# A fused Fourier filter and MLP kernel: d transform split by the parity of d, W staged raw and copied forwards and backwards on chip

One core of one Trainium2 chip. The metric is the device time of one execution in microseconds (us). "Span" is the part of it between the first and the last instruction of the profile; the rest, about 1.7 us (135.18 - 133.5 in the profiled run of the kernel before), lies outside. A core alone has no second die to compare with; a run counts as slow when it is over 1.5% above the fastest of the same kernel.

## What must be computed

```python
def reference(A_x, A_w_r, A_w_i, B_x, B_w1, B_b1, B_w2, gate_w):   # x: 1 x 2048 x 512, bf16
    x = A_x
    g = sigmoid((x * gate_w).sum(-1, keepdims=True))
    a = irfft2(rfft2(x) * (w_r + 1j * w_i))          # w_r, w_i: 2048 x 257
    h = x @ w1 + b1                                  # w1: 512 x 1792
    b = (h * tanh(softplus(h))) @ w2                 # w2: 1792 x 512
    return g * a + (1 - g) * b
```

The program is two jobs that share the engines: a Fourier chain and an MLP. The Fourier chain is: t transform by 16 x 128 in two steps (s1, s2), d transform (a1), product with W, and the same backwards (s2i, s1i, a1i). Between s1/a1 and s2, and again between s2i and s1i, the data go through a scratch array in DRAM. The two MLP products are mm1 (x by w1) and mm2 (by w2).

## The kernel before

A list scheduler fixes the order on every engine when the kernel is built, from guessed durations. A task is taken when its inputs are guessed to be ready, highest priority first. So an input that lands later than guessed stops the engine although other work is ready. All loads but one tiny one are issued from SyncE (queue "sp").

```python
def dma(name, dst, src, nbytes, reads=(), writes=(), deps=(), ..., queue="sp", bw=DMA_BW):
    t = G.add(name, [(queue, 0.46, lambda e: e.dma_start(dst, src))], reads=reads, writes=writes, deps=deps, ...)
    t.xfer = nbytes / bw            # the guess of the transfer's time

ld_x(0, 1, bw=600e3); ld_x(1, 2, bw=260e3)
ld_w1(0)                            # 256 columns of w1
ld_x(2, 4, bw=290e3)
ld_w1(1)                            # 256 more
ld_c(0, ...); ld_w1(2); ...         # tables, and the other 1280 columns

def wload(nm, dst, src_t, o, h, deps=()):          # half h of w_r or w_i
    v = src_t.rearrange("(g h e2 j) k -> g h e2 j k", g=16, h=2, e2=2)
    part("p", 0, dst[0:32, j0:j0 + n, :]..., v[:, 0, :, j0:j0 + n, :]..., 32 * 514 * n, 188e3)
    # ... the mirrored rows: 16 partitions each, rows of 257 elements in reverse order
wload("wr", Wa, A_w_r, "Wa", 0); wload("wi", Wb, A_w_i, "Wb", 0)
# after the first scratch writes are issued:
wload("wr", Wa, A_w_r, "Wa", 1, t_r1w); wload("wi", Wb, A_w_i, "Wb", 1, t_r1w)

def f_a1(e, t=t, sl=sl):                           # forward d transform of one tile
    e.matmul(o[:, :, 1::2, :], In1[:, t, 256:384], f4(256), start=True, stop=False)   # 256 columns
    e.matmul(o[:, :, 1::2, :], In1[:, t, 384:512], f4(512), start=False, stop=True)   # 256
    e.matmul(o[:, :, 0, :], In1[:, t, 0:128], f2(0), start=True, stop=True)           # 128
    return e.matmul(o[:, :, 2, :], In1[:, t, 128:256], f2(128), start=True, stop=True)  # 128
```

Note the source of the forward W load: its outermost dimension has 16 entries (g).

Of the kernel before, what the change touches and what calls it, by code (L numbers as in the profile page):

```python
# [7 lines left out]
BF = mybir.dt.bfloat16  # L8
# [9 lines left out]
NWARM = 14  # L18
# [5 lines left out]
BIDX = {t: i for i, t in enumerate(BGRP)}  # L24
# [7 lines left out]
def _bf16_bits(a):  # L32
# [8 lines left out]
        "SA0", "SA1", "SB0", "SB1", "SA0e", "SA1e", "SB0e", "SB1e")  # L41


def _pin(t, pl, c, e2):
    return t * 8 + pl * 4 + c * 2 + e2


def _pout(co, sg, g, e2):


    return co * 64 + (32 + 31 - g * 2 - e2 if sg else g * 2 + e2)


def _stage2():
    t = np.arange(16)
    w = lambda num, den: np.exp(-2j * np.pi * num / den)
    M = {n: np.zeros((128, 128)) for n in MATS}

    def put_c(mat, po, rows, vals):

        mat[rows, po[0]] += vals.real
        mat[rows, po[1]] += vals.imag

    for e2 in range(2):
        Rr, Ri, Ir, Ii = (_pin(t, pl, c, e2) for pl in (0, 1) for c in (0, 1))
        for g in range(16):
            wt = w(t * g, 16)
            po = [[(_pout(0, sg, g, e2), _pout(1, sg, g, e2)) for sg in range(2)]][0]
            for mat, ok in (("RF", True), ("RFe", e2 == 1)):
                if ok:  # L70
                    m = M[mat]
                    put_c(m, po[0], Rr, wt)
                    put_c(m, po[0], Ri, 1j * wt)
                    put_c(m, po[0], Ir, 1j * wt)
                    put_c(m, po[0], Ii, -wt)
                    cw = np.conj(wt)
                    put_c(m, po[1], Rr, cw)
                    put_c(m, po[1], Ri, -1j * cw)
                    put_c(m, po[1], Ir, 1j * cw)
                    put_c(m, po[1], Ii, cw)  # L80
            for mat, ok in (("RFz", True), ("RFez", e2 == 1)):
                if ok:
                    m = M[mat]
                    put_c(m, po[0], Rr, wt)
                    put_c(m, po[0], Ri, 1j * wt)
                    put_c(m, po[1], Ir, wt)
                    put_c(m, po[1], Ii, 1j * wt)
            if e2 == 0:
                w64 = w(64 * t, 2048) * w(t * (15 - g), 16)
                m = M["RFe"]  # L90
                put_c(m, po[0], Rr, wt)
                put_c(m, po[0], Ir, 1j * wt)
                put_c(m, po[1], Ri, w64)
                put_c(m, po[1], Ii, 1j * w64)
                m = M["RFez"]
                for x, (r0, r64) in enumerate(((Rr, Ri), (Ir, Ii))):
                    if g == 0:
                        m[r0, po[x][0]] += 1.0
                        m[r0, po[x][1]] += w(t * 8, 16).real
                    elif g < 8:  # L100
                        put_c(m, po[x], r0, wt)
                    else:
                        put_c(m, po[x], r64, w(64 * t, 2048) * w(t * (g - 8), 16))

    inv = {}
    for nm in ("", "e", "z", "ez"):
        inv[nm] = np.zeros((128, 128))

    def take(mat, po, col, vals):

        mat[po[0], col] += vals.real
        mat[po[1], col] += -vals.imag

    for e2 in range(2):
        Rr, Ri, Ir, Ii = (_pin(t, pl, c, e2) for pl in (0, 1) for c in (0, 1))
        for g in range(16):
            wt = np.conj(w(t * g, 16))
            po = [(_pout(0, sg, g, e2), _pout(1, sg, g, e2)) for sg in range(2)]
            for nm, ok in (("", True), ("e", e2 == 1)):
                if ok:  # L120
                    m = inv[nm]
                    take(m, po[0], Rr, wt / 2)
                    take(m, po[0], Ri, -1j * wt / 2)
                    take(m, po[0], Ir, -1j * wt / 2)
                    take(m, po[0], Ii, -wt / 2)
                    cw = np.conj(wt)
                    take(m, po[1], Rr, cw / 2)
                    take(m, po[1], Ri, 1j * cw / 2)
                    take(m, po[1], Ir, -1j * cw / 2)
                    take(m, po[1], Ii, cw / 2)  # L130
            for nm, ok in (("z", True), ("ez", e2 == 1)):
                if ok:
                    m = inv[nm]
                    take(m, po[0], Rr, wt)
                    take(m, po[0], Ri, -1j * wt)
                    take(m, po[1], Ir, wt)
                    take(m, po[1], Ii, -1j * wt)
            if e2 == 0:
                w64 = np.conj(w(64 * t, 2048) * w(t * (15 - g), 16))
                m = inv["e"]  # L140
                take(m, po[0], Rr, wt)
                take(m, po[0], Ir, -1j * wt)
                take(m, po[1], Ri, w64)
                take(m, po[1], Ii, -1j * w64)
                m = inv["ez"]
                for x, (r0, r64) in enumerate(((Rr, Ri), (Ir, Ii))):
                    if g == 0:
                        m[po[x][0], r0] += 1.0
                        m[po[x][1], r0] += w(t * 8, 16).real
                    elif g < 8:  # L150
                        take(m, po[x], r0, 2 * wt)
                    else:
                        take(m, po[x], r64, 2 * np.conj(w(64 * t, 2048)) * np.conj(w(t * (g - 8), 16)))
    for nm in ("", "e", "z", "ez"):
        m1 = inv[nm]
        M["RI1" + nm] = m1
        if "z" in nm:
            M["RI2" + nm] = np.concatenate([m1[64:128], m1[0:64]])

    for co in range(2):  # L160
        for e2 in range(2):
            for g in range(16):
                for x in range(2):
                    po = _pout(co, x, g, e2)
                    for suf in ("", "e"):
                        A, B = M[f"SA{x}{suf}"], M[f"SB{x}{suf}"]
                        if suf == "" or e2 == 1:
                            A[_pout(co, 0, g, e2), po] += 0.5
                            A[_pout(co, 1, g, e2), po] += 0.5
                            B[_pout(co, 0, g, e2), po] += 0.5  # L170
                            B[_pout(co, 1, g, e2), po] -= 0.5
                        elif g == 0:
                            A[_pout(co, 0, 8 * co, 0), po] += 1.0
                        elif g < 8:
                            A[_pout(co, 0, g, 0), po] += 0.5
                            A[_pout(co, 0, 16 - g, 0), po] += 0.5
                            B[_pout(co, 0, g, 0), po] += 0.5
                            B[_pout(co, 0, 16 - g, 0), po] -= 0.5
                        else:
                            h = g - 8  # L180
                            A[_pout(co, 1, 15 - h, 0), po] += 0.5
                            A[_pout(co, 1, h, 0), po] += 0.5
                            B[_pout(co, 1, 15 - h, 0), po] += 0.5
                            B[_pout(co, 1, h, 0), po] -= 0.5
    return np.stack([M[n] for n in MATS], axis=1)


def _build_consts():
    cs = {}
    n = np.arange(128)[:, None]  # L190
    q = np.arange(64)[None, :]

    def trig(nn, k):
        th = 2 * np.pi * nn * k / D
        return np.cos(th), -np.sin(th)

    c0, s0 = trig(n, 4 * q)
    s0[:, 0] = (-1.0) ** np.arange(128)
    c2, s2 = trig(n, 4 * q + 2)
    ko = np.concatenate([4 * q + 1, 4 * q + 3], axis=1)  # L200
    blocks = [c0, s0, c2, s2]
    for h in range(2):
        c1, s1 = trig(n + 128 * h, ko)
        blocks += [c1, s1]
    cs["FD"] = np.concatenate(blocks, axis=1)
# [3 lines left out]
    FT = np.zeros((128, NT, 128))  # L209
    GT = np.zeros((128, NT, 128))  # L210
    for t in range(NT):
        th = 2 * np.pi * e * (16 * p + t) / S
        FT[:, t, 0:64] = np.cos(th)
        FT[:, t, 64:128] = -np.sin(th)
        FT[:, t, 64] = (-1.0) ** p[:, 0]
        GT[0:64, t, :] = 2 * np.cos(th).T
        GT[64:128, t, :] = -2 * np.sin(th).T
        GT[0, t, :] = 1.0
        GT[64, t, :] = (-1.0) ** p[:, 0]
    cs["CF"] = np.concatenate([cs.pop("FD"), FT.reshape(128, NT * 128)], axis=1)  # L220
    cs["GT"] = GT


    GD = np.zeros((128, 768))
    n1, n2 = np.arange(128)[None, :], np.arange(256)[None, :]
    for i in range(2):
# [826 lines left out]
```

## Time and profile before

| | before |
|---|---|
| time, median of 3 runs | 135.45 us |
| span of the profiled run | 133.5 us |
| TensorE (PE) busy | 128.9 us, 97% |
| idle time of PE in the span | 4.6 us |
| longest waits of PE | 1.2 us (warm-up, on zeros), 0.6 us |
| first mm1 matmul | 6.70 us |
| first matmul of s2 / of s1i | 45.48 / 92.39 us |

Two things that the prediction does not show matter later. This is the view of the transfers of the kernel before: out<-in, queue, number, size, median us from issue to landing.

```profile
scr<-R SPq DMA_DIRECT2D x8, 512.0 KB, 4.0
...
w_sb<-in_B_w_dram SPq DMA_DIRECT2D x2, 256.0 KB, 3.9
```

The two first pieces of w1 land 3.9 us after their issue, and the scratch writes after 4.0. This is the timeline of SyncE in the middle: start, length, what.

```profile
27.84 4.73 SPq L495 DMA_DIRECT2D scr<-R  x3
32.61 1.95 SPq L495 DMA_DIRECT2D w_sb<-in_B_w_dram  x2
36.35 2.19 SPq L495 DMA_DIRECT2D R<-scr  x4
```

Both halves of w2 are issued by 34.6 us, ahead of the second half of W.

### The profile page before, as it was taken

Reading aid. Unit: us, or ns where it says so; the run is one execution under the profiler, and the core shown is the slowest. Engines: PE = TensorE matmul, PEld = TensorE weight load, DVE = VectorE, ACT = ScalarE, POOL = GpSimd, SP = SyncE. Lnnn points to the kernel's source line nnn. Section 1 sums busy time; section 2 is a strip of 40 time slices with the busy share of each in tenths; the row PEclk is TensorE's granted clock in tenths of the full one; section 3 lists DMA queues with packets and bytes.
Section 4 is the critical chain, followed back from the end, with each engine's and each line's share of the span. In section 5 each row is a group of like instructions: output and inputs, shape, how many; then the busy total and the mean of one; then the engine's idle time right before and its main releaser. Section 6 shows DMA issues by size and latency. Waiting matters only on the chain.

```text
span 133.5 us, 2357 instructions
## 1 busy us (share of the span) xinstructions
PE 128.9 (97%) x813; PEld 69.4 (52%) x813; DVE 99.4 (75%) x241; ACT 82.8 (62%) x145; POOL 4.7 (4%) x8
## 2 busy tenths in 40 slices
PE   6999999999999999999998999999999999999991
PEld 2489565675444444444443444445666566565451
DVE  0558868487999799999999995001899999977822
ACT  3199788896774156756167898778887654552000
POOL 2000000000002900000000000000000000000000
PEclk9999999999999999999999999999999999999999
DMA  3999999997999999947100840399311222220121
GB/s 89 289 382 401 329 187 158 190 333 230 254 352 394 383 166 125 140 100 206 49 0 0 323 158 0 158 258 290 80 46 37 79 79 79 79 85 1 43 75 39
DMA packets 25015, 22.24 MB, mean 167 GB/s; under 512 B 7596, under 2 KB 21420, under 8 KB 24876
## 3 DMA queue, kind: packets, MB, share of 16 engines
q1 hardware_dynamic: 24976, 22.10, 62.2%
q8 instruction: 6, 0.10, 0.3%
q14 instruction: 5, 0.04, 0.1%
q10 hardware_dynamic: 28, 0.00, 0.0%
HBM read 14.23 MB, written 6.29 MB: 154 GB/s over the span
## 4 chain that ended last, share of the span: by engine, by line
PE 45%; DVE 5%; issue 1%; ACT 0%; ACTq 0%
PE ps L858 18%; PE ps L836 18%; PE ps L885 3%; PE ps L903 1%; PE ps L904 1%; PE ps L905 1%; PE ps L809 1%; DVE PX L794 1%; DVE PX L793 1%; DVE Wb L692 1%; DVE PX L790 1%; DVE PX L797 1%; PE ps L780 1%; DVE R L520 1%; ACT PX L521 0%
## 5 line engine op out<-in xcount | busy, mean ns | idle before, releaser
L836 PE MATMUL ps<-xT,w_sb 128*128 128x512 bf16 (+1 forms) x240 | 52.3, 365 | 0.1
L858 PE MATMUL ps<-w_sb,hsb 128*128 128x512 bf16 (+2 forms) x238 | 52.3, 366 | 0.0
L845 ACT ACTIVATE hsb<-ps,b1f 128x512 bf16<-128x512 f32 (+1 forms) x60 | 38.9, 660 | 9.4 <-PE ps L836 9.4
L858 PEld LDWEIGHTS ps<-w_sb,hsb 128*128 128x128 bf16 x238 | 22.3, 98 | 22.9
L836 PEld LDWEIGHTS ps<-xT,w_sb 128*128 128x128 bf16 x240 | 22.7, 98 | 22.0 <-issue 0.6
L520 DVE CAST R<-ps 128x512 bf16<-128x512 f32 (+1 forms) x23 | 15.4, 689 | 6.6 <-PE ps L656 3.7
L521 ACT ACTIVATE R<-ps 128x512 bf16<-128x512 f32 (+1 forms) x25 | 14.4, 595 | 3.1 <-PE ps L809 2.1
L869 ACT ACTIVATE R<-ps,omg 128x512 bf16<-128x512 f32 x12 | 8.1, 687 | 9.2 <-PE ps L858 8.1
L521 ACT ACTIVATE PX<-ps 128x512 bf16<-128x512 f32 x15 | 8.9, 596 | 6.9 <-PE ps L779 4.1
L699 DVE SCALAR_TENSOR_TENSOR R<-R,gwb 128x512 bf16<-128x512 bf16 x16 | 9.9, 687 | 0.2 <-DVE R L520 0.2
L909 ACT ACTIVATE PX<-ps,gcol 128x128 f32<-128x128 f32 x15 | 5.4, 364 | 5.7 <-PE ps L905 5.7
L892 DVE CAST TT<-ps 128x512 bf16<-128x512 f32 x2 | 1.3, 687 | 9.9 <-PE ps L885 9.9
L895 ACT ACTIVATE TT<-ps 128x512 bf16<-128x512 f32 x14 | 8.3, 593 | 0.2 <-PE ps L885 0.2
L797 DVE TENSOR_TENSOR PX<-PX 128x512 bf16<-128x512 bf16 x16 | 6.8, 424 | 1.0
L793 DVE TENSOR_TENSOR PX<-PX,Wb 64x512 bf16<-64x512 bf16 x16 | 6.7, 421 | 0.5
L794 DVE TENSOR_TENSOR PX<-PX,Wb 64x512 bf16<-64x512 bf16 x16 | 6.7, 420 | 0.2
L790 DVE TENSOR_TENSOR PX<-PX,Wa 128x512 bf16<-128x512 bf16 x16 | 6.8, 423 | 0.1
L538 PE MATMUL ps<-GD 128*128 128x512 bf16 x14 | 5.6, 527 | 1.2 <-DVE GD L535 1.2
L809 PE MATMUL ps<-PX,SM 128*128 128x512 bf16 x15 | 5.7, 380 | 0.6 <-ACT PX L521 0.6
L925 DVE SCALAR_TENSOR_TENSOR PX<-ps,gcol,PX 128x256 bf16<-128x256 f32 x12 | 5.8, 484 | 0.5
L937 DVE SCALAR_TENSOR_TENSOR R<-ps,omg,R 128x512 bf16<-128x512 f32 (+2 forms) x5 | 3.2, 645 | 3.9 <-PE ps L858 3.9
L931 DVE TENSOR_TENSOR R<-R,PX 128x512 bf16<-128x512 bf16 x12 | 5.1, 426 | 1.2 <-ACT R L869 0.8
(98 smaller groups left out, 127.9 us busy)
## 6 DMA issues: line engine op xcount, KB each, us to landing
scr<-R SPq DMA_DIRECT2D x8, 512.0 KB, 4.0
R<-scr SPq DMA_DIRECT2D x8, 512.0 KB, 7.4
w_sb<-in_B_w_dram SPq DMA_DIRECT2D x2, 896.0 KB, 7.8
out_dram<-R SPq DMA_DIRECT2D x7, 256.0 KB, 2.0
R<-in_A_x_dram SPq DMA_DIRECT2D x3, 512.0 KB, 9.6
w_sb<-in_B_w_dram SPq DMA_DIRECT2D x1, 1280.0 KB, 7.7
SM<-c_sm SPq DMA_DIRECT2D x1, 576.0 KB, 6.3
Wa<-in_A_w_r_dram SPq DMA_DIRECT2D x2, 257.0 KB, 8.1
```

Source lines behind the costliest of these rows:

```text
L520: t = G.add(name, [("dve", dve_dur(n), lambda e: e.tensor_copy(out=outf(), in_=inf())), ("act", act_dur(n), lambda e: e.activation(outf(), ...
L521: ("act", act_dur(n), lambda e: e.activation(outf(), inf(), AF.Copy))],
L699: t_gx.append(G.add(f"gx{t}", [("dve", 0.72, lambda e, t=t: e.scalar_tensor_tensor(out=x_sb[:, t, :], in0=x_sb[:, t, :], scalar=1.0, in1=g ...
L790: return e.tensor_tensor(out=v(P1, sP, 0, 128), in0=v(Xb, sX, 0, 128), in1=Wa[:, js, 0:256], op=ALU.mult)
L793: e.tensor_tensor(out=v(P2, sQ, 0, 64), in0=v(Xb, sX, 64, 128), in1=Wb[64:128, js, 0:256], op=ALU.mult)
L794: return e.tensor_tensor(out=v(P2, sQ, 64, 128), in0=v(Xb, sX, 0, 64), in1=Wb[0:64, js, 0:256], op=ALU.mult)
L797: return e.tensor_tensor(out=P1[:, sP.i, :], in0=P1[:, sP.i, :], in1=P2[:, sQ.i, :], op=ALU.add)
L836: ins = e.matmul(ps[:, bk(sl), cols], w1_sb[:, dt_, 128 * ft:128 * (ft + 1)], xT[:, dt_, 4 * c + h0:4 * c + h1, :], start=(dt_ == 0), stop ...
L845: return e.activation(hsb[:, hb, ft, cols], ps[:, bk(sl), cols], AF.Mish, bias=b1f[:, ft:ft + 1])
L858: ins = e.matmul(ps[:, bk(sl), 0:n1 - n0], hsb[:, hb, ft, 128 * tl:128 * (tl + 1)], w2_sb[:, ft, n0:n1], start=(ft == 0), stop=(ft == NFT ...
L869: G.add(f"bev_{t}", [("act", act_dur(512, True), lambda e, t=t, sl=sl: e.activation(ya[:, t, :], ps[:, bk(sl), :], AF.Copy, scale=omg[:, t ...
L895: return e.activation(TT[:, st.i, :, :].rearrange("p a b -> p (a b)"), ps[:, bk(sk), :], AF.Copy)
```

## The change

Its intent is less work on TensorE. The d axis is split into even and odd d. Frequency k and 256-k are then sums and differences of the same two halves, and that combination is folded into the matrices of the t transform, which cost PE the same as before (s1: 64 matmuls, 4.7 us busy in both kernels). So the d transform becomes four 128-column matmuls a tile in place of 256 + 256 + 128 + 128. The price is that W is wanted twice, once forwards and once with k reversed. It is loaded raw into a staging area (a part of the tensor hsb, so the profile shows these loads as hsb<-in_A_w_r and hsb<-in_A_w_i) and copied on chip in both directions. The order of the loads at the start and in the middle changes too.

```diff
-NWARM = 14                     # 512 columns each
+NWARM = 15                     # 256 columns each
@@ forward d transform
-e.matmul(o[:, :, 1::2, :], In1[:, t, 256:384], f4(256), ...)   # and three more
+for i in range(4):
+    ins = e.matmul(ps[:, bk(sl), 128*i:128*(i+1)], In1[:, t, 128*i:128*(i+1)], FD[:, 128*i:128*(i+1)], start=True, stop=True)
@@ start
-ld_x(0, 1, bw=600e3); ld_x(1, 2, bw=260e3); ld_w1(0); ld_x(2, 4, bw=290e3); ld_w1(1)
+ld_x(0, 2, bw=400e3); ld_w1(0); ld_x(2, 4); ld_w1(1)
 def ld_w1(h):
-    dma(f"ld_w1_{h}", w1_sb[:, :, f0:f1], w1v[:, :, f0:f1], ..., bw=bw)
+    dma(f"ld_w1_{h}", w1_sb[:, :, f0:f1], w1v[:, :, f0:f1], ..., bw=bw, queue="act" if h < 2 else "sp", prio=...)
@@ W, staged raw: w = 0 is w_r, 1 is w_i
+def wload(w, src_t, deps=()):
+    src = lambda r0, *ap: bass.AP(src_t.tensor, src_t.offset + r0 * 257, [list(a) for a in ap])
+    G_ = (128 * 257, 16)
+    S2 = bass.AP(S_.tensor, S_.offset, [[2 * row, 64], [1, 16 * 257]])
+    part(0, S2, src(0, (16 * 257, 4), G_, (1, 16 * 257)), 64 * 8224, 300e3)     # the forward load, 514 KB
+    for bb in (0, 2, 1, 3):                                                      # the mirrored rows
+        part(1 + bb, dst(32 * bb + 1, 16, e0, 16 - e0), src(128 - 16 * bb - e0, G_, (-257, 16 - e0), (1, 257)), ..., 150e3)
+wload(0, A_w_r); ld_w2(0)               # early
+wload(1, A_w_i, t_e2); ld_sm; ld_w2(1, t_e2)   # after the forward d transform
@@ W, copied on chip: v = 0 forwards, 1 with k reversed
+for w in range(2):
+    for bb in range(4):
+        for v in range(2):
+            i = SW[32*bb:32*bb+32, w, :, 0:130]
+            if v: i = bass.AP(i.tensor, i.offset + 256, [i.ap[0], [257, 16], [-1, 130]])
+            # copy to WW[32*v:32*v+32, w, 16*bb:16*bb+16, :], on DVE or ACT
@@ ... transform matrices, scratch layout (rows of 256 B in the reads), inverse d transform,
@@ ... gated sum: one 256-column ACT copy and two 256-column DVE operations a tile
```

## The prediction

> **What bounds the kernel now.** I read the page's busy shares and slices first, then the chain of waits, the timeline by engine, and a table of stretches.
>
> ```profile
> PE 128.9 (97%) x813; PEld 69.4 (52%) x813; DVE 99.4 (75%) x241; ACT 82.8 (62%) x145; POOL 4.7 (4%) x8
> ...
> PE   6999999999999999999998999999999999999991
> ...
> DVE  0558868487999799999999995001899999977822
> ```
>
> TensorE (PE) is never short of work. The MLP matmuls (mm1, L836; mm2, L858) fill every gap that the Fourier chain leaves. DVE is full only between 30 and 83 us, is empty around 85 to 92 us, and is full again after. The chain of waits (start, length, what) and PE's timeline give the rates:
>
> ```profile
> 82.19 10.36 PE ps L836 x48
> ...
> 121.69 9.12 PE ps L858 x56
> 130.83 0.35 DVE R L937
> ```
>
> ```profile
> 6.70 1.03 PE L836 MATMUL ps<-xT,w_sb 128*128 128x256 bf16 x8
> ...
> 28.05 0.27 PE L668 MATMUL ps<-CF,R 128*128 128x256 bf16 x1
> 28.16 0.27 PE L669 MATMUL ps<-CF,R 128*128 128x256 bf16 x1
> 28.27 0.22 PE L670 MATMUL ps<-CF,R 128*128 128x128 bf16 x1
> 28.33 0.22 PE L671 MATMUL ps<-CF,R 128*128 128x128 bf16 x1
> 28.39 0.27 PE L668 MATMUL ps<-CF,R 128*128 128x256 bf16 x1
> ...
> 121.53 9.26 PE L858 MATMUL ps<-w_sb,hsb 128*128 128x512 bf16 x56
> ```
>
> The reader is to see three things. A 512-column matmul costs 10.36/48 = 0.216 us, a 256-column one 0.11 us and a 128-column one 0.055 us (differences of starts; the 0.27 and 0.22 are latencies). Real work starts at 6.70 us; before it PE warms up on zeros and does 8 transposes. And after the last inverse d transform, at 121.5 us, PE still has 9.1 us of mm2 to do: the Fourier chain is some 9 us ahead of where it would set the end. So the time is start (6.7) + PE work + PE's gaps + a tail of 2.7 us (last matmul at 130.8 to 133.5), plus 135.45 - 133.5 = 1.95 us outside the span.
>
> PE work after 6.70: mm1 208 x 0.216 + 32 x 0.11 = 48.4; mm2 the same columns, 48.4; the four t and 2048/128 stages (s1, s2, s2i, s1i) 3.55 + 3.45 + 3.45 + 3.55 = 14.0; forward d transform a1 16 x 0.33 = 5.3; inverse a1i 5.3; transposes and tables 0.9. Sum 122.3, in 124.1 us. Gaps are about 1.8 us.
>
> [...]0.216 at 512, 0.055 at 128, so four 128-column matmuls are not penalised for being narrow, even with a weight load for each. [...]4112 elements in 1.23 us is 3.3 per ns[...]. No run shows step -1. [...]0.43 to 0.50 us an issue on SyncE.
>
> **The change, part by part.**
>
> (a) *a1 and a1i*: 256+256+128+128 columns become 4 x 128. Per tile 0.33 becomes 4 x 0.055 = 0.22, so 0.11 x 32 tiles = **3.5 us less PE work**. All on the path, since PE is the bound. Columns of s1, s2, s2i, s1i are unchanged; z, table and uz matmuls grow from 32 to 64 columns, under 0.2 us. Stationary operands are now read with a stride of two elements in s1; s1i has strided ones already and its weight loads are 104 against 98 ns, hidden.
>
> (b) *Start*: x tiles 0-1 come in one DMA and tiles 2-3 in the next, the first two w1 pieces are issued from ACT at the same time, and the warm-up shrinks from 14 x 512 to 15 x 256 columns. Four to five SyncE issues of 0.45 us stood in line before; w1's first piece goes out about 0.3 us earlier, x tiles 2-3 about 0.9 us earlier. In the first 6.7 us the queues moved 89 and then 291 GB/s, where 370 is reached later, so there is room. I take **0.9 us** (0.4 to 1.3) off the start.
>
> (c) *DVE, forward*: two of four butterflies go, 4 x 0.29 + 6 x 0.42 = 3.7 us. *DVE, end*: the two 128-wide f32 operations per tile (L916) go, 32 x 0.345 = 11.0 us busy; ACT's gated copy doubles, 15 x 0.11 = 1.6 us. *DVE, middle*: W copies. Sixteen copies of 32 x 2080 are new; [...]0.69 us each, **11 us**; the four sign copies stay at 1.23.
>
> ```profile
> L692 DVE TENSOR_SCALAR Wb<-Wb 64x4112 bf16<-64x4112 bf16 x2 | 2.5, 1232 | 0.0
> ...
> L916 DVE SCALAR_TENSOR_TENSOR PX<-ps,gcol,PX 128x128 f32<-128x128 f32 x16 | 5.5, 345 | 0.0
> ```
>
> (d) *The middle's timing.* This stretch table (PE, PEld, DVE, ACT, POOL busy, clock, DMA share, GB/s) is the one to follow:
>
> ```profile
> 36.30:45.30 9.00, 9.00 (x44) 4.05 (x42) 8.51 (x23) 4.26 (x7) 2.65 (x1) 1.00 1.05 381
> 45.30:82.90 37.60, 37.04 (x185) 16.51 (x184) 33.96 (x81) 25.13 (x43) 1.28 (x1) 1.00 0.62 126
> 82.90:92.40 9.50, 9.50 (x46) 4.33 (x45) 0.01 (x1) 7.55 (x11) 0.00 (x0) 1.00 0.75 217
> ```
>
> 45.3 to 82.9 is the W product, bound by DVE (34 of 37.6 us). Before it, 36.3 to 45.3 is the read back from scratch at full DMA rate; after it, 82.9 to 92.4 is the second round trip. Gate products hold DVE until about 42 us; then the new copies come in line: 8 x 0.69 + 2 x 1.23 = 8.0 us for w_r, again 8.0 for w_i, and the first product needs both. So products start near 54 us instead of 46.5; the second half's 2.5 us of sign copies inside the stretch is gone, so it ends about 5 us later, near 87. Scratch reads now come in 256 B pieces[...]. The inverse t transform then starts at 99 to 100 instead of 92.4 us: **7 us of the 9 us slack are spent**. But the last stage is shorter: per tile DVE's 1.89 us (94.84 to 96.83 and on) falls to about 1.24, 16 x 0.65 = 10 us back, so DVE no longer paces it. PE has enough to fill with: mm1 of chunks 2 and 3 and mm2, 24 + 44 = 68 us of it after 45 us. Result: PE stays the bound, with perhaps 0.5 us more of gaps, since the order of work on PE is fixed when the kernel is built.
>
> Sum: 135.45 - 3.5 - 0.9 + 0.5 - 0.2 (smaller table stage gaps, the 0.56 us wait at 71 us moves) = **131.3 us**, 3.1% faster.
>
> **Rivals.**
>
> *1: the reversed copies are not fast.* [...]Half could go to ACT. [...]PE, in fixed order, waits at the products: 135 to 141 us. [...]L790 to L794 read W rows of 257 elements, every other one misaligned, at the full 0.42 us. One in six.
>
> *2: the first read back is late.* w_i, the stage matrices and half of w2 (2.4 MB, half of w_i in 514 B pieces) queue before it, against 1.8 MB before. At 16.6 to 22.4 us W loads and transposes made only 180 GB/s with the queues full. If it lands at 56 instead of 50 and the fixed order expects it sooner, PE waits 1 to 4 us: 132 to 135 us. One in four.
>
> *3: less at the start.* Loads are limited by bytes, not issues; then (b) gives 0 to 0.3 us[...]: 132.0 us.
>
> *4: more than counted.* DVE relief lets PE's gaps vanish (1.8 us) and the start gains 1.3: 129.5 us.
>
> **Range and chances.** The 3.5 us is certain while PE is the bound; the start adds 0 to 1.3, the gaps take 0 to 3. The middle of that is 131.3; eight in ten lie in 129.7 to 134.2. The 2% lines are 132.74 and 138.2. Rivals 1 and the worse half of 2 lead above the first: faster 0.74, same 0.20, slower 0.06.
>
> **What would show it.** Right: PE busy down by about 5 us with share still 96% or more; a1 and a1i tiles 0.22 us apart; first mm1 near 5.8 us; forward and reversed W copies both near 0.7 us; DVE near 99.4 - 3.7 - 11 + 11 = 96 us; inverse stage begins near 99 us and mm2 runs on alone at the end for over 2 us. Wrong: PE waits of over 1 us at the products or at the inverse t transform, reversed copies over 1 us, or the end set by DVE rather than by mm2.

## The result

The changed kernel is **slower**: 144.08 us median of 4 runs (141.77 and 143.79, and 144.37 and 145.87, which counted as slow) against 135.46. A ratio here is the mean time of one kernel's fast runs over the mean of the other's fast runs of the same rounds, so not quite the ratio of the medians. It is 1.054, with a 95% interval of 1.041 to 1.067. From here on, lines of the changed kernel have their own numbers: mm1 is L821, mm2 L843, a1 L636, a1i L888, s1i L870, and every DMA is L465. In e2, e3 and e4 those of the matmuls are one higher.

Page of the changed kernel:

```profile
PE 127.5 (90%) x800; PEld 68.4 (48%) x814; DVE 96.7 (68%) x213; ACT 89.0 (63%) x146; POOL 4.3 (3%) x8
...
PE   6574899999999906999999999999999999999992
...
PEclk9999999999999997799999999999999999999999
DMA  3999937999942896973446007210399722221021
```

PE's busy time fell by 1.4 us, yet its share fell from 97 to 90%: it is idle for 14.6 us in a span of 142.1, against 4.6. The row in tenths has two holes: one in the first 18 us and one in the slices from 50 to 57 us, with a fallen clock right after (0.50 from 56 to 58 us). The waits name both (what waited on what: us in total, times, longest):

```profile
PE ps L843 <- DMA w_sb<-in_B_w_dram: 4.6, 1, 4.6
...
PE ps L821 <- DMA w_sb<-in_B_w_dram: 4.1, 2, 2.2
```

PE waits 4.1 us for w1 and 4.6 us for w2, 8.7 of the 10.0 us of added idle time. The timeline of PE puts them in place (in brackets: idle before, and what ended it):

```profile
8.04 1.01 PE L821 MATMUL ps<-xT,w_sb 128*128 128x256 bf16 x4 [2.19 <-DMA w_sb<-in_B_w_dram]
...
12.66 0.61 PE L821 MATMUL ps<-xT,w_sb 128*128 128x256 bf16 x4 [1.91 <-DMA w_sb<-in_B_w_dram]
...
46.75 3.19 PE L843 MATMUL ps<-w_sb,hsb 128*128 128x512 bf16 x13
54.58 1.82 PE L843 MATMUL ps<-w_sb,hsb 128*128 128x512 bf16 x5 [4.65 <-DMA w_sb<-in_B_w_dram]
...
117.22 1.67 PE L843 MATMUL ps<-w_sb,hsb 128*128 128x512 bf16 x7
118.73 0.39 PE L888 MATMUL ps<-GD,TT 128*128 128x128 bf16 x4
118.95 0.39 PE L870 MATMUL ps<-CF,R 128*128 128x128 bf16 x4
```

The last two rows show that the arithmetic of the change works: four 128-column matmuls of a1i start at 118.73 and the next group at 118.95, so 0.22 us a tile. The second half of w2 explains itself in SyncE's timeline of the changed kernel:

```profile
29.36 4.00 SPq L465 DMA_DIRECT2D scr<-R  x4
33.41 11.81 SPq L465 DMA_DIRECT2D hsb<-in_A_w_i_dram  x6
45.27 0.59 SPq L465 DMA_DIRECT2D w_sb<-in_B_w_dram  x1
46.87 9.16 SPq L465 DMA_DIRECT2D R<-scr  x5
```

Six issues for w_i hold SyncE for 11.81 us. Issuing them should take 6 x 0.6: that is the length of their shortest (0.62). One of the six takes 7.77 us. The second half of w2 stands behind them, goes out at 45.27 us and lands at 54.58. The DMA row (tenths of 16 engines' time) has a 2 in the slice from 42.6 to 46.2 us, at 95 GB/s, while SyncE is stuck. So work is queued and yet the DMA engines are three quarters idle: asked of 43 to 45 us alone, the profile gives a share of 0.25, which is 4 of 16. The packet records of the trace say the same: in these 2 us four packets are under way at almost every moment.

### The profile page after: what moved, and what is told of

Its sections match the earlier page's. It is cut to its first block, busy times and chain, and to the rows that moved or that the text cites. A ratio compares the mean times of both kernels' runs of the same rounds, so it can differ in the third digit from the quotient of the medians.

```text
span 142.1 us, 2309 instructions
## 1 busy us (share of the span) xinstructions
PE 127.5 (90%) x800; PEld 68.4 (48%) x814; DVE 96.7 (68%) x213; ACT 89.0 (63%) x146; POOL 4.3 (3%) x8
## 2 busy tenths in 40 slices
DMA packets 33136, 22.01 MB, mean 155 GB/s; under 512 B 24037, under 2 KB 29413, under 8 KB 32997
## 4 chain that ended last, share of the span: by engine, by line
PE 47%; DVE 21%; DMA 14%; SPq 8%; issue 4%; ACT 3%; ACTq 1%; DVEq 0%
PE ps L843 20%; PE ps L821 16%; DMA w_sb<-in_B_w_dram 14%; SPq L465 8%; DVE PX L775 4%; DVE PX L774 4%; DVE PX L771 3%; DVE PX L778 3%; PE ps L888 3%; PE ps L870 3%; ACT R L491 2%; DVE R L490 2%; PE ps L625 2%; DVE WW L669 2%; PE ps L636 1%
## 5 line engine op out<-in xcount | busy, mean ns | idle before, releaser
L843 PE MATMUL ps<-w_sb,hsb 128*128 128x512 bf16 (+2 forms) x231 | 52.6, 375 | 5.0 <-DMA w_sb<-in_B_w_dram 4.6
L821 PE MATMUL ps<-xT,w_sb 128*128 128x512 bf16 (+1 forms) x233 | 52.8, 369 | 4.9 <-DMA w_sb<-in_B_w_dram 4.1
L830 ACT ACTIVATE hsb<-ps,b1f 128x512 bf16<-128x512 f32 (+1 forms) x60 | 38.4, 662 | 11.1 <-PE ps L821 11.0
L843 PEld LDWEIGHTS ps<-w_sb,hsb 128*128 128x128 bf16 x238 | 22.7, 100 | 29.2 <-DMA w_sb<-in_B_w_dram 5.1
L821 PEld LDWEIGHTS ps<-xT,w_sb 128*128 128x128 bf16 x240 | 23.0, 99 | 28.1 <-issue 2.6
L490 DVE CAST R<-ps 128x512 bf16<-128x512 f32 (+1 forms) x22 | 14.6, 687 | 7.6 <-PE ps L625 5.7
L666 ACT ACTIVATE WW<-hsb 32x2080 bf16<-32x2080 bf16 x4 | 7.8, 1938 | 4.1 <-DMA hsb<-in_A_w_i_dram 3.8
L665 DVE COPY WW<-hsb 32x2080 bf16<-32x2080 bf16 x12 | 8.4, 696 | 2.7 <-DMA hsb<-in_A_w_i_dram 2.4
L895 ACT ACTIVATE PX<-ps,gcol 128x256 f32<-128x256 f32 x14 | 6.3, 472 | 4.6 <-PE ps L888 4.6
L877 DVE CAST TT<-ps 128x512 bf16<-128x512 f32 x3 | 2.0, 688 | 9.9 <-PE ps L870 9.9
L880 ACT ACTIVATE TT<-ps 128x512 bf16<-128x512 f32 x13 | 7.3, 595 | 0.0
L774 DVE TENSOR_TENSOR PX<-PX,WW 64x512 bf16<-64x512 bf16 x16 | 6.7, 421 | 0.5
L775 DVE TENSOR_TENSOR PX<-PX,WW 64x512 bf16<-64x512 bf16 x16 | 6.7, 419 | 0.2
L771 DVE TENSOR_TENSOR PX<-PX,WW 128x512 bf16<-128x512 bf16 x16 | 6.7, 420 | 0.2
```

The costliest lines, as they stand in the source:

```text
L490: t = G.add(name, [("dve", dve_dur(n), lambda e: e.tensor_copy(out=outf(), in_=inf())), ("act", act_dur(n), lambda e: e.activation(outf(), ...
L665: t_wc.append(G.add(f"wv{w}{bb}{v}", [("dve", dve_dur(2080, 4), lambda e, wv=wv: e.tensor_copy(**wv())), ("act", act_dur(2080), lambda e, ...
L771: return e.tensor_tensor(out=v(P1, sP, 0, 128), in0=v(Xb, sX, 0, 128), in1=Wa[:, js, 0:128], op=ALU.mult)
L774: e.tensor_tensor(out=v(P2, sQ, 0, 64), in0=v(Xb, sX, 64, 128), in1=Wb[64:128, js, 0:128], op=ALU.mult)
L775: return e.tensor_tensor(out=v(P2, sQ, 64, 128), in0=v(Xb, sX, 0, 64), in1=Wb[0:64, js, 0:128], op=ALU.mult)
L821: ins = e.matmul(ps[:, bk(sl), cols], w1_sb[:, dt_, 128 * ft:128 * (ft + 1)], xT[:, dt_, 4 * c + h0:4 * c + h1, :], start=(dt_ == 0), stop ...
```

## The experiments

Each ran beside runs of the kernel before on the same chip, which took 134.5 to 135.8 us every time; e5_again, e2_again and e6 were on another chip than the rest. The two theories to be told apart were these. **A**: the pieces of w1 come late because they are issued from ACT's queue. **B**: the forward load of each W is put on few DMA engines (four packets under way, share 0.25), because its source's slowest dimension is 4, where the kernel before has 16. Rivals: more bytes in 256 B and 514 B pieces (my prediction's view), or a change of order alone (half of w2 now stands behind w_i).

### e1: w1 back on SyncE's queue

```diff
-queue="act" if h < 2 else "sp"
+queue="sp"
```

> The changed kernel with one thing undone: the first two w1 pieces are issued from SyncE again, between the x loads, as before the change. Theory A ([...]they landed at 8.0 and 12.6 us and PE waited): first MLP matmul at or before 6.8 us, no PE wait over 1 us before 16 us, and 3 to 5 us off the changed kernel, so 139 to 141 us, with the wait for the second half of w2 near 50 us still there. Rival A' (the first 13 us are limited by bytes, whatever queue they are on; 400 GB/s were moved): PE still waits, under 1.5 us gained.

Measured: 144.67 us (142.88 to 145.26), ratio 1.064 [1.053, 1.076]. The size expected was missed. The first mm1 came right, at 5.34 us, and no wait on w1 is left among PE's waits. A new one of 1.7 us is there instead, on the table CF for s1 (`PE ps L625 <- DMA CF<-c_cf`), against "no PE wait over 1 us before 16 us". And:

```profile
PE ps L843 <- DMA w_sb<-in_B_w_dram: 9.4, 1, 9.4
```

The wait on w2 grew from 4.6 to 9.4 us. The second half of w2 is issued at 46.51 us, and PE goes on at 55.21 (45.27 and 54.58 in the changed kernel), though PE was earlier before it. An earlier start alone is worth nothing: it is waited away in the middle.

### e2: the forward W load spread over sixteen rows

```diff
-part(0, S2, src(0, (16 * 257, 4), G_, (1, 16 * 257)), 64 * 8224, 300e3)
+for bb in range(4):       # 16 partitions each; the source's outermost dimension is now 16
+    part(6 + bb, bass.AP(S_.tensor, S_.offset + 32*bb*row, [[2*row, 16], [1, 16*257]]), src(16*bb, G_, (1, 16*257)), 16 * 8224, 300e3)
```

> The changed kernel with the 514 KB forward load of each W split into four loads of 16 partitions, whose source has 16 as its outermost count, instead of one whose source has 4. Theory B (the outermost count of 4 keeps that load on 4 of the 16 DMA engines, and everything queued behind it waits for these 4): DMA share no longer near 0.25 around 40 to 46 us, landings of the W pieces fall from 15 to under 10 us, the second half of w2 lands 5 us or more earlier, the PE wait of 4.65 us near 50 us is gone, and 4 to 6 us off the changed kernel: 138 to 140 us. Rival B' (the 514 B reversed rows, or the order of loads, are what clogs): landings stay at 12 us or more and under 2 us gained.

The copies wait for the piece that they read (part of the edit, not shown). Measured: 135.28, 139.14, 134.92 and 139.64 us. The two fast runs give a ratio of 0.999 [0.992, 1.006]; the upper two counted as slow, at full clock (1.00). The profile is of a fast run. SyncE's timeline and PE's timeline of it, in turn:

```profile
30.07 6.41 SPq L465 DMA_DIRECT2D hsb<-in_A_w_i_dram  x9
36.52 0.58 SPq L465 DMA_DIRECT2D w_sb<-in_B_w_dram  x1
38.12 10.56 SPq L465 DMA_DIRECT2D R<-scr  x8
```

```profile
6.99 0.60 PE L822 MATMUL ps<-xT,w_sb 128*128 128x256 bf16 x4 [1.42 <-DMA w_sb<-in_B_w_dram]
...
10.63 0.61 PE L822 MATMUL ps<-xT,w_sb 128*128 128x256 bf16 x4 [2.16 <-DMA w_sb<-in_B_w_dram]
```

Nine issues now take 6.41 us instead of six taking 11.81. The pieces of W (both halves) land 3.0 to 7.1 us after issue (14.1 to 16.5 before the edit), w2 goes out 8.75 us earlier, and PE's wait on it is gone. The waits on w1 stay, 3.6 us in all. So the load's shape (B) is a cause. Bytes and order by themselves do not make the wait, since e2 has both as the changed kernel has them. A is left for the rest.

### e4: the same load on two rows

The edit also splits the load, so a control was wanted: two loads, each with a slowest source dimension of 2.

```diff
-part(0, S2, src(0, (16 * 257, 4), G_, (1, 16 * 257)), 64 * 8224, 300e3)
+for hb2 in range(2):
+    part(6 + hb2, bass.AP(S_.tensor, S_.offset + 64*hb2*row, [[2*row, 32], [1, 16*257]]), src(32*hb2, (16*257, 2), G_, (1, 16*257)), 32 * 8224, 300e3)
```

> Control for the split: the forward load of each W in two loads of 32 partitions, whose source has 2 as its outermost count. Theory B: each is on 2 of 16 engines, DMA share falls to near 0.13 while one is alone, the waits near 50 us get longer by 4 us or more: 147 us or more. If splitting as such is what helps, it is faster than the changed kernel.

Measured: 150.05 us, one run, so its state is unknown. SyncE's timeline, then the DMA row of its page:

```profile
36.73 15.33 SPq L465 DMA_DIRECT2D hsb<-in_A_w_i_dram  x7
52.10 0.58 SPq L465 DMA_DIRECT2D w_sb<-in_B_w_dram  x1
```

```profile
DMA  4999952189952159595444401530379911312021
```

PE waits 12.1 us for w2. While the W loads run alone, the row shows 1 (slices from 26.0 to 29.7 and from 48.2 to 51.9 us, 60 and 54 GB/s) where the changed kernel shows 2 to 3 (90 and 95 GB/s). Asked of 49 to 52 us alone, the profile of e4 gives a share of 0.12, 2 of 16, and the packet records show two packets under way at almost every moment, where the changed kernel had four. Slowest dimension 2, 4, 16 gives 150.1 us (one run), 142.8 and 135.1 (means of fast runs; the medians of all are 144.1 and 137.2): the order of B. Splitting by itself does not help. A split into four loads that each keep a dimension of 4 was not run.

### e3: both edits

> Both of the former two. If A and B are the two whole causes, the losses add: 9 to 11 us off the changed kernel, 133 to 135 us, about the kernel before. If the 3.5 us of saved matmul time and the shorter start were also as predicted, it reaches 131.5 to 132.5. If one hides behind the other, it is near the better of the two single ones.

Measured: 132.47 us (131.78 to 133.05, all fast), ratio 0.980 [0.974, 0.985]. Its page and PE's timeline:

```profile
PE 125.1 (96%) x814; PEld 67.3 (51%) x814; DVE 96.7 (74%) x213; ACT 88.8 (68%) x146; POOL 4.3 (3%) x8
```

```profile
5.71 0.71 PE L822 MATMUL ps<-xT,w_sb 128*128 128x256 bf16 x4
...
118.07 0.61 PE L889 MATMUL ps<-GD,TT 128*128 128x128 bf16 x8
118.51 9.26 PE L844 MATMUL ps<-w_sb,hsb 128*128 128x512 bf16 x56
```

Both waits are gone, s2 starts at 47.93 us (59.36 in the changed kernel), s1i at 96.26 (107.83), and mm2 runs on alone for the last 9.3 us as in the kernel before. Repeated with five rounds:

> e3_both once more, with five rounds: both faults of the loads taken out. If the earlier 0.980 holds, 132.0 to 133.0 us and a ratio of 0.975 to 0.985 to the kernel before. If that was a lucky set of runs (e2_rows_on_16 has two modes 4 us apart), some runs fall at 135 us or above.

Measured: 132.54 us (132.03 to 133.59), ratio 0.980 [0.976, 0.984]. So the first value was no luck; it sits on the 2% line, and the verdict stays unclear by a hair.

### b1: the ACT queue in the kernel before

The cleanest test of A: the kernel before, with nothing but its first two w1 pieces on ACT's queue (at the priority that they have in the changed kernel).

> The kernel before, with only its first two pieces of w1 issued from ScalarE's queue instead of SyncE's; nothing of the d transform changed. Theory[...]: TensorE waits 3 to 5 us in all on the w1 pieces in its first 13 us, the second piece lands after 10 us, and the time is 138.5 to 140.5 us. Rival (the start was late in the changed kernel because of its own bytes and order, not of the queue): waits on w1 stay under 1.5 us and the time within 1 us of the kernel before.

Measured: 137.46 us (137.02 to 137.62, all fast), ratio 1.015 [1.011, 1.019]. The transfers, then PE's timeline:

```profile
w_sb<-in_B_w_dram ACTq DMA_DIRECT2D x2, 256.0 KB, 7.5
```

```profile
8.93 1.03 PE L836 MATMUL ps<-xT,w_sb 128*128 128x256 bf16 x8 [1.38 <-DMA w_sb<-in_B_w_dram]
```

By the 2% line this is "same", but the interval lies above 1. Neither expectation fits in size. The landing takes 7.5 us instead of 3.9, mm1 starts 2.2 us later (8.93 against 6.70), and the time grows by 2.0. So A is real in a kernel in which nothing else was touched, at half the size I gave it. The wait itself is only 1.4 us, because PE filled part of the delay with warm-up matmuls (seven in 2.46 us from 4.86) and transposes.

### e5: one load of w1 with longer rows, still on ACT's queue

Why are they late? One reading (A1) was the size of the rows, 512 B beside 2 KB and more; the other (A2) was the queue, whatever its rows. This keeps e2 and makes one load of 512 KB with rows of 1 KB.

```diff
-f0, f1, bw = ((0, 256, 250e3), (256, 512, 280e3), (512, F, 370e3))[h]
+f0, f1, bw = ((0, 512, 250e3), None, (512, F, 370e3))[h]       # ld_w1(1) is dropped
```

> The changed kernel with the forward W loads spread over 16 rows of partitions (as in e2_rows_on_16) and the two first w1 pieces, still on ScalarE's queue, made one load of 512 KB with rows of 1 KB instead of two loads of 256 KB with rows of 512 B. Theory A1[...]: all 512 columns are there by 7.3 to 9 us, the second wait of TensorE on w1 is gone, and the time is about 2 us under e2_rows_on_16 (134 to 136 us). Rival A2[...]: the load lands at 10.5 us or later, TensorE waits 4 us or more for it in one piece, and the time is 138 us or more.

Measured: 137.7, 135.9, 132.04, 132.04 and 132.21 us; the first two counted as slow, and the fast three give 0.976 [0.970, 0.981], unclear. The profile fell on the slowest run. Its timeline and its table of stretches (busy times of PE, PEld, DVE, ACT, POOL, then clock, DMA share, GB/s):

```profile
10.44 1.86 PE L821 MATMUL ps<-xT,w_sb 128*128 128x256 bf16 x8 [5.11 <-DMA w_sb<-in_B_w_dram]
```

```profile
6.70:13.00 6.30, 2.56 (x17) 2.07 (x18) 0.23 (x1) 0.95 (x2) 0.00 (x0) 0.63 1.03 405
```

That is about A2's landing, 8.8 us after issue, in one run, and better than A1's time in three others. Repeated:

> e5_rows16_w1_merged once more, since its profile fell on its slowest run (137.7 us, w1 there at 10.44 us, clock 0.63 after it) and three others took 132.0 to 132.2 us. Theory[...]: a profile of a fast run shows the merged w1 load at TensorE by 7 to 8.5 us, the wait on it under 3 us, and everything after the start the same; the runs spread over 4 us or more again. Rival (the modes come from later, not from the start): a fast profile shows the same late w1 and has its gain elsewhere.

Measured: 133.78, 134.59, 136.07 and 133.83 us, ratio 0.993 [0.988, 0.998]; in the profile, of a fast run, the load lands 5.5 us after issue and mm1 starts at 7.12. So the landing of a load on the second queue moved by over 3 us between the two profiles (which were on two chips), and the time with it. The spread of "4 us or more again" did not come: it was 2.3. With e2 again:

> e2_rows_on_16 once more, whose runs fell at 135 and at 139 us with a profile only of the fast ones (waits on w1 of 3.6 us). Theory: two modes again, within 1 us of 135 and 139 us; if the profile falls on a slow one, its waits on w1 are 7 us or more and the rest unchanged. Rival: a slow profile shows the extra 4 us in the middle.

Measured: 136.75, 137.04, 134.82 and 137.29 us, ratio 1.004 [0.997, 1.012], not two clean modes at 135 and 139. In the profile (136.75) the first w1 piece comes in time and the second 2.65 us late, at 10.45. The expectation of two fixed modes fell; what is shown is a spread of 2.3 to 5.7 us in the runs of the changed kernel, e2 and e5, which have w1 on ACT's queue, and of 1.3 to 2.0 us in e3 and e6, which have not. But e1, with all on SyncE's queue, spread by 2.4 us, and b1, with w1 on ACT's, by only 0.6: the queue alone does not set the spread. Row size as the reason is not shown.

### e6: the merged w1 load on SyncE's queue

> e3_both with the two first w1 pieces made one load of 512 KB, on SyncE's queue. Theory: [...]runs spread under 1.5 us and none is over 133.5 us; the load is there by 6.5 to 7.5 us (later than e3_both's first piece, sooner than its second plus the wait), so the time is 131.8 to 133 us, within 0.5 us of e3_both. Rival (merging by itself causes the spread of e5_rows16_w1_merged): runs at 135 us or above here too.

Measured: 131.43 us (131.04, 131.15, 131.16, 131.70, and two slow at 133.02 and 133.06), ratio **0.971 [0.968, 0.974], faster**. It is the best of all and beats both kernels. The spread was 2.0 us, not under 1.5. The profile is of a slow run (131.3 us span). In it the load landed 4.8 us after issue, and mm1 starts at 6.13 us with a wait of 0.56 us (put down to DVE, not to the load), but its first eight matmuls take 1.86 us, where the changed order on SyncE in e3 took 1.04 for eight. The traces show such a pace at the start and after long waits. In the changed kernel four such matmuls took 1.01 us at 8.04 us and 0.61 at 12.66, and the clock records begin between them, at 10.8 us (at 5.4 in the kernel before, 6.0 in e3). After 4.65 us of idling there, five matmuls took 1.82 us, where seven took 1.67 later, and the granted clock was 0.85 in 54.6 to 66 us; in e5, after 5.11 us, it was 0.63 in 6.7 to 13 us. For e6 the page's clock row reads 9 throughout, but the clock records begin only at 10.1 us, and the pace changes about there: eight such matmuls took 1.86 us at 6.13, 1.34 at 9.50 and 1.04 at 12.01. So a slow clock until then is an estimate from the pace; no record shows it. That the two slow runs of e6 are this and nothing else is likely, not shown, since no fast run of it was profiled; nor did any run change the shorter warm-up.

## Why the prediction was wrong

The mechanism that it promised was there; two transfers that it passed over took more than it gave. By its own steps:

**(a) a1 and a1i, 3.5 us off PE.** Right in its mechanism: 0.22 us a tile as written. PE's busy time falls 3.8 us once the waits are out (125.1 in e3), not the "about 5" of its list, and 1.0 of that lies before the first mm1, where the warm-up is shorter; from the first mm1 on it falls 2.8 (123.4 to 120.6). In the changed kernel only 1.4 show. The other 2.4 us are put down to matmuls at a lower clock after the waits (0.85 in 54.6 to 66 us; 203 of mm2's took 389 ns each, against 379 in e3); no run separates them.

**(b) start, 0.9 us gained.** Wrong, and this is one of the two steps that failed: it counted ACT's queue as issue time saved and nothing else (0.3 us for w1's first piece). The first mm1 is at 8.04 us instead of the 5.8 predicted, and the second piece is there at 12.66. With the pieces on SyncE the start gains 1.0 us (5.71 in e3), as the sum had it. So the order and the paired x loads were worth what was said, though a wait on the table CF that was not there before takes some back (0.4 us in e3, 1.0 in its repeat); ACT's queue cost 2.0 us where it was tried alone (b1), and 2.6 us between the fast runs of e2 and those of e3 (135.10 and 132.5).

**(c) the copies.** Right, and rival 1 is dead; its 135 to 141 us were my estimate, and this trace shows no slow reversed copy. The groups of the changed kernel (busy, mean ns):

```profile
L666 ACT ACTIVATE WW<-hsb 32x2080 bf16<-32x2080 bf16 x4 | 7.8, 1938 | 4.1 <-DMA hsb<-in_A_w_i_dram 3.8
L665 DVE COPY WW<-hsb 32x2080 bf16<-32x2080 bf16 x12 | 8.4, 696 | 2.7 <-DMA hsb<-in_A_w_i_dram 2.4
```

Twelve copies ran on DVE in 0.69 to 0.70 us each, forwards and reversed alike (eight copies of each kind exist, so at least four of the twelve are reversed), against 0.69 predicted; four went to ACT at 1.94 us. DVE is at 96.7 us, against 96.

**(d) the middle's timing.** This is the step that failed most, with its rival 2, "the first read back is late". That rival was seen, for the right queue, but put down to bytes ("2.4 MB ... against 1.8 MB"), and given one in four and 1 to 4 us. It was not bytes: e2 moves the same 22.01 MB. It was the 514 KB forward load, whose source's slowest dimension is 4. It ran at a quarter of the DMA engines (share 0.25), everything issued behind it waited, and SyncE itself was held for 11.81 us. What came late first was not the read back, either, but the second half of w2: the order on SyncE had moved it behind w_i. PE waited 4.65 us and then ran mm2 at a lower clock (0.50 from 56 to 58 us); s2 started at 59.36 us, where rival 2 has the read back landing at "56 instead of 50". Spreading the load alone is worth 7.7 us by the means of fast runs (142.8 of the changed kernel, 135.1 of e2) and 6.9 by the medians of all. A run with w2 issued ahead of w_i again, and the load left as it is, was not made.

In e3 the step's own numbers come out within a few us, on the early side: s2 at 47.93 (50), s1i at 96.26 (99 to 100), mm2 alone at the end for 9.3 us ("over 2"). That is partly luck. The 1.89 us of DVE a tile holds from the second tile on; the two times that it names lie 1.99 apart. Its terms for the products add up to 58 (42 + 8 + 8), not to the "near 54" that it wrote, and the first product came at 49.02: the copies began at 37.2, four of the sixteen went to ACT, and the first product did not wait for the last copies of w_i. The second read back, in 256 B pieces, ran at about 218 GB/s in e3 against 290 in 512 B pieces before, and its transfers took 9.4 us instead of 6.8, 2.6 more; s1i started before they were all there.

**The sum.** 131.3 us was predicted. With both loads mended it is 132.5 (e3) and 131.4 (e6, which also merges two loads, so that its nearness to the sum is partly luck). The 1.95 us outside the span set the median of the runs against the span of a faster one; within one run it is 1.7 us, which does not touch the sum. The 0.5 us allowed for gaps was too little in e3: PE is idle for 5.6 us of the span, 1.0 more than before.

What stays open: why a load on the second queue lands late and at such different times. b1 and the e5 runs show that it does, and that row size alone does not settle it. Open too is whether the shorter warm-up costs time.

## What to carry to other kernels

Before a large load is re-cut, look at the slowest dimension of its source: here a 4 where a 16 stood left one 514 KB load at a DMA share of 0.25, and it held up the transfers behind it and the engine that issues them (11.8 us over six issues, against 6.4 over nine with 16). Look for it in the trace as a low DMA share while the queue's issues grow long, and not in the byte count. Where the order on the engines is fixed when the kernel is built, put the loads that the first matmuls wait for on the queue that was seen to land them early (here SyncE's: 3.9 us against 7.5 from ACT's in b1), and take out all late transfers together: e1 shows that mending the first alone only makes the second longer (9.4 us instead of 4.6).
